# Attention pairs 3 and 4 take the VectorE turn: three pairs in place of five keep the turn on TensorE

## The chip, the cores and the metric

The kernel runs on one core of one Trainium2 chip. The metric is the time of one execution on the device, in microseconds. Three runs of the kernel before gave 651.52, 655.0 and 658.75 us; the median is 655.0 us. Besides, one execution was profiled; every row of a trace below is from that one.

## The reference

Rotary attention over 8 batches of 8 heads, 576 positions and a head width of 64, and behind it a gated feed-forward layer over the 512 features of the eight heads:

```python
q_rot, k_rot = (rotate(q), rotate(k))
scores = scale * np.matmul(q_rot, k_rot.transpose(0, 1, 3, 2))
scores = scores - np.max(scores, axis=-1, keepdims=True)
attn = np.exp(scores)
attn = attn / (np.sum(attn, axis=-1, keepdims=True) + 1e-09)
x = np.matmul(attn, v)          # the eight heads side by side: (8, 576, 512)
...
for k in range(5):              # causal taps of width 5
    gate_pre += conv_w[k][None, None, :] * xp[:, k:k + S, :]
gate = 1.0 / (1.0 + np.exp(-gate_pre))
val = x @ w_val
return (gate * val @ w_out).astype(np.float32)
```

The factors of the matrix products are split into a high and a low part, so that three products of reduced precision stand for one of float32.

## The kernel before

**Work and tiles.** Two heads make a pair; there are 32 pairs, four to a batch. A pair's steps are: load q and k (`load`, L198); rope as two multiplications by the tables and an addition (`rope_mul` L212, `rope_add` L216), then a high part on ScalarE (L223) and a low part (`qk_lo`, L227); five groups of scores on TensorE (`s_mm`, L255: four groups of 128 query rows for both heads, and one of the last 64 rows of both heads mixed, for which `q_mixed` lays out the queries); the maxima on VectorE (L261, nine) and the exponentials on ScalarE (L274, nine); the turn of the weights, so that keys lie on partitions; the product of weights and V (`pv_last` L359, `pv_mm` L369, L374, L377); the norm (`x_norm`, L405), for which reciprocal sums (L386) go out to memory and come back (L392 to L401); the high and low parts of the result (L412, L416), four taps on VectorE (L429) and one on ScalarE, and the gate (L433).

**The turn, in two kinds.** A pair p below `EARLY` (L31), and the last pair, turn on TensorE: eight groups of four transposes (`t_mm`, L303) and their edges (`th_mm`, L316), each copied out of PSUM by ScalarE (L190) or VectorE (L192). The other pairs turn on VectorE: four transposes of 32x32 blocks (`turn`, L289), and 16 DMAs on SP's queue which bring the blocks to their places (`move`, L294). The two lines that choose:

```python
ph = "e" if p < EARLY else ""
cs = TURNED.get(p, (0, 1, 2, 3) if p >= EARLY and not last else ())
```

**Feed-forward.** When the four pairs of a batch are there, two products follow (`f_mm`, L463, 192 matmuls in all for a batch), with the gate (L468) and a split (L472, L476) between them and an output copy (L482 or L484) and DMA behind them. Its weights arrive as float64 bits; eight blocks are decoded once, early on, with six steps of which five are VectorE's (L497 to L504), three matmuls (L539 to L541) and copies.

**Buffers.** PSUM holds three score buffers of two banks (`ps_s`) and two banks for all else (`ps_t`). Three buffers `big` hold turned weights, blocks on their way and raw feed-forward weights.

**What sets the order.** Every step is a job with a due time: a base (18.5 us times p, plus the step's place) plus an entry of the table `DUE`. The planner (`Plan.order`) takes the ready job with the least due time whose buffers are free. Jobs then stand on their engine's queue in that order and run in it. `PICK` gives the engine of a step where there is a choice (V VectorE, A ScalarE, G GpSimd). Early pairs have keys of their own in both tables, with an "e" behind. Where a GpSimd job follows a VectorE job which uses the port that the two share, `Plan.run` adds a wait on that job.

Of the kernel before, what the change touches and what calls it, by code (L numbers as in the profile page):

```python
# [30 lines left out]
EARLY = 5  # L31
# [113 lines left out]
def attn_gated_ffn(ctx: ExitStack, tc: tile.TileContext, q2, k2, v2, tab, w_val, conv_w, w_out, out, collect=None):  # L145
# [410 lines left out]
    def at(key, base, e, ns, fn, *args, pick=None, r="", w="", kb=0, mode=None, port=False):  # L556

        options = ns if pick else None
        if pick:
            e = PICK.get(pick, e)  # L560
            ns, port = options[e]
            args = [ENG[e] if a == "ENGINE" else a for a in args]
        plan.add(base + DUE.get(key, 0.0), e, fn, *args, r=r, w=w, port=port)
        if collect is not None:
            collect.append((key, base, pick, options, ns, kb * (3.6 if fn is move else 2.95), mode, port or e == "G"))

    def toks(f, *ranges):
        out = [f]
        for r in ranges:
            out = [x.replace("@", str(v), 1) for x in out for v in r]  # L570
        return " ".join(out)
# [30 lines left out]
    for p in range(NP):  # L602
        t = PERIOD * p
        par = p % 2
        last = p == NP - 1
        ph = "e" if p < EARLY else ""
        cs = TURNED.get(p, (0, 1, 2, 3) if p >= EARLY and not last else ())
        xt = toks(f"x{par}#@", range(5))
# [200 lines left out]
```

## Time and profile before

| | |
|---|---|
| median of three runs | 655.0 us (651.52 to 658.75) |
| the profiled execution | 652.48 us, of which the span of its instructions 650.7 us |
| TensorE, matmuls | 616.9 us busy (95% of the span) |
| VectorE | 579.1 us (89%) |
| ScalarE | 462.7 us (71%) |
| GpSimd | 390.3 us (60%) |
| DMA | 134.43 MB |
| granted TensorE clock, mean | 0.996 of full speed |

A share is an average over stages with different limits, so the rows below are read by stretch. Matmuls are pipelined and their ends are modelled; a busy TensorE need not be at its peak. Overlapping records count once in a busy time, so the mean of a step can be more than its share of the busy time.

### The profile page before, as it was taken

The page shows a single profiled execution, that of the slowest core. Times are in us where ns is not written, and L with a number is a line of the kernel's source. Part 1 is how long each engine was busy: PE and PEld are TensorE (multiplying, and loading weights), DVE is VectorE, ACT ScalarE, POOL GpSimd, SP SyncE. Part 2 cuts the span into 40 slices and gives each one's busy share as a digit, 9 for nine tenths or more (in the row PEclk, how much of TensorE's full clock was granted, in tenths as well). Part 3 has the DMA queues.
Part 4 walks back from the last instruction along what each step waited for, and adds up shares of the span by engine and source line. Part 5 has one row for each costly group of instructions (what it writes and reads, how often), then busy time and mean ns, then how long its engine had stood idle before and what let it go on. Part 6 is the DMA issues. An engine that isn't in the chain of part 4 may idle for free.

```text
span 650.7 us, 15423 instructions
## 1 busy us (share of the span) xinstructions
PE 616.9 (95%) x5683; PEld 503.4 (77%) x5683; DVE 579.1 (89%) x827; ACT 462.7 (71%) x1161; POOL 390.3 (60%) x297
## 2 busy tenths in 40 slices
PE   8899988989899998999999999999999999999997
PEld 7666665678677886888778787888788877788797
DVE  6898999998899999999999999999999999995453
ACT  4788888867777777767877777767777777664521
POOL 1322446776777868687677868766976867630200
PEclk9899999999999999999999999999999999999999
DMA  5524432378989989999999999989999898864102
GB/s 185 225 78 153 162 117 101 114 206 242 268 235 260 258 250 250 263 241 252 239 249 252 241 262 255 267 241 256 254 263 254 233 252 210 249 166 132 56 2 74
DMA packets 51482, 134.43 MB, mean 207 GB/s; under 512 B 10928, under 2 KB 20944, under 8 KB 51408
## 3 DMA queue, kind: packets, MB, share of 16 engines
q1 hardware_dynamic: 50864, 132.86, 72.8%
q8 instruction: 45, 0.74, 0.5%
q10 hardware_dynamic: 544, 0.59, 0.3%
q14 instruction: 29, 0.24, 0.1%
HBM read 62.48 MB, written 9.59 MB: 111 GB/s over the span
## 4 chain that ended last, share of the span: by engine, by line
PE 49%; DVE 23%; DMA 9%; ACT 6%; issue 4%; POOL 4%; SPq 3%; ACTq 0%; DVEq 0%; POOLq 0%
PE ps_t L463 17%; PE ps_t L369 12%; PE ps_s L255 10%; DVE nm L261 8%; DVE big L289 7%; DMA big<-big 5%; DVE g L429 3%; SPq L294 3%; ACT p L274 3%; PE ps_t L359 3%; PE ps_t L303 2%; PE ps_t L374 2%; PE ps_t L330 1%; ACT big L190 1%; DVE g L468 1%
## 5 line engine op out<-in xcount | busy, mean ns | idle before, releaser
L261 DVE TENSOR_REDUCE nm<-ps_s 128x1 f32<-128x576 f32 x288 | 201.8, 741 | 19.9 <-PE ps_s L255 18.8
L274 ACT ACTIVATE p<-ps_s,nm 128x576 f32<-128x576 f32 x256 | 187.7, 738 | 39.5 <-DVE nm L261 38.4
L255 PE MATMUL ps_s<-k,q 64*128 64x288 f32 x1536 | 145.0, 310 | 11.4 <-ACT p L274 9.2
L255 PEld LDWEIGHTS ps_s<-k,q 64*128 64x128 f32 x1536 | 111.0, 184 | 37.6 <-ACT p L274 18.2
L289 DVE STREAM_TRANSPOSE big<-p 128x1152 f32<-128x1152 f32 x104 | 139.8, 1357 | 0.0
L429 DVE SCALAR_TENSOR_TENSOR g<-x,cw,g 128x576 f32<-128x576 f32 (+1 forms) x132 | 122.4, 927 | 0.9 <-ACT g L426 0.6
L369 PE MATMUL ps_t<-big,v 128*64 128x256 f32 (+2 forms) x1024 | 118.4, 382 | 0.0
L227 POOL TENSOR_TENSOR q<-iq,q 128x576 fp32r<-128x576 f32 (+2 forms) x33 | 48.8, 1477 | 94.9 <-ACT q L223 89.8
L369 PEld LDWEIGHTS ps_t<-big,v 128*64 128x64 f32 x1024 | 70.1, 137 | 44.1 <-issue 13.5
L212 POOL TENSOR_TENSOR iq<-iq,tab 128x576 f32<-128x576 f32 x54 | 77.1, 1450 | 19.8 <-DMA iq<-in_q 13.3
L463 PE MATMUL ps_t<-yh,wout_hi 128*128 128x288 f32 x256 | 79.2, 310 | 0.0
L463 PE MATMUL ps_t<-xh,wval_hi 128*128 128x288 f32 x256 | 79.0, 309 | 0.0
L463 PE MATMUL ps_t<-yl,wout_hi 128*128 128x288 f32 x256 | 76.2, 298 | 1.9 <-POOL yl L476 1.9
L463 PE MATMUL ps_t<-xl,wval_hi 128*128 128x288 f32 x256 | 76.3, 298 | 0.0
L463 PE MATMUL ps_t<-xh,wval_lo 128*128 128x288 f32 x256 | 75.9, 297 | 0.0
L463 PE MATMUL ps_t<-yh,wout_lo 128*128 128x288 f32 x256 | 75.5, 295 | 0.0
L227 POOL TENSOR_TENSOR k<-ik,k 128x576 fp32r<-128x576 f32 x31 | 52.5, 1694 | 37.4 <-DVE iq L212 25.0
L476 POOL TENSOR_TENSOR yl<-g,yh 128x288 fp32r<-128x288 f32 x56 | 46.7, 841 | 43.5 <-ACT yh L472 41.2
L416 POOL TENSOR_TENSOR xl<-x,xh 128x576 fp32r<-128x576 f32 (+1 forms) x32 | 47.6, 1487 | 25.5 <-PE ps_t L463 13.4
L463 PEld LDWEIGHTS ps_t<-xh,wval_hi 128*128 128x128 f32 x256 | 48.7, 190 | 2.8 <-issue 1.6
L472 ACT CAST yh<-g 128x288 fp32r<-128x288 f32 x64 | 26.6, 431 | 33.9 <-DVE g L468 33.9
L463 PEld LDWEIGHTS ps_t<-yl,wout_hi 128*128 128x128 f32 x256 | 48.3, 189 | 3.1 <-POOL yl L476 3.0
(95 smaller groups left out, 1107.9 us busy)
## 6 DMA issues: line engine op xcount, KB each, us to landing
big<-big SPq DMA_DIRECT2D x416, 144.0 KB
ik<-in_k SPq DMA_DIRECT2D x31, 576.0 KB
iq<-in_q SPq DMA_DIRECT2D x31, 576.0 KB
v<-in_v SPq DMA_DIRECT2D x32, 320.0 KB
rb<-rd SPq DMA_DIRECT2D x64, 144.0 KB
out_t<-oo SPq DMA_DIRECT2D x64, 144.0 KB
big<-in_w_val SPq DMA_DIRECT2D x4, 512.0 KB
big<-in_w_out SPq DMA_DIRECT2D x4, 512.0 KB
```

The source lines that it names most:

```text
L212: eng.tensor_tensor(out=t[:, i, a:b], in0=t[:, i, a:b], in1=tabs[:, i, a:b], op=ALU.mult)
L227: eng.tensor_tensor(out=t[:, 1], in0=state[p][n + "in"][:, 0, a:b], in1=t[:, 0].bitcast(F32), op=ALU.subtract)
L255: T.matmul(out=ps[:, half, 0:288], lhsT=st["q"][rows, x, c * 128:c * 128 + 128] if c < 4 else mixq[p % 2][:, x], rhs=st["k"][rows, y, k0:k ...
L261: V.tensor_reduce(out=st[f"nm{i}"], in_=st[f"s{i}"], axis=AX.XY, op=ALU.max, negate=True)
L274: A.activation(out=pd.rearrange("p (b x) -> p b x", b=2), in_=st[f"s{i}"], func=AF.Exp, bias=st[f"nm{i}"], scale=1.0, accum_out=sums[p % 2 ...
L289: V.transpose(out=t[:, :, cs.index(c)].rearrange("p b k i -> p k b i"), in_=st[f"p{c}"].rearrange("p h s -> p (h s)").rearrange("p (k b i) ...
L369: T.matmul(out=acc[HEAD[h], 0:n], lhsT=st["v"][:, j, h, :], rhs=st["pt"][:, :, c0:c1, 5 * place(p, 2 * c0 + h) + j].rearrange("p a c i -> ...
L416: eng.tensor_tensor(out=st["xl"][:, a:b], in0=xs[p % 2][:, 4 + a:4 + b], in1=st["xh"][:, a:b].bitcast(F32), op=ALU.subtract)
L429: V.scalar_tensor_tensor(out=g, in0=x_sb[:, a + k:b + k], scalar=w, in1=g, op0=ALU.mult, op1=ALU.add)
L463: T.matmul(out=acc[:, 0:n], lhsT=wt[w][:, kc, ds], rhs=mv, start=(kc == 0 and i == 0), stop=(kc == NCH - 1 and i == 2))
L472: A.copy(out=ffn[b, "h", dc, lo], in_=ffn[b, "y", dc, lo])
L476: eng.tensor_tensor(out=ffn[b, "l", dc, lo], in0=y, in1=ffn[b, "h", dc, lo].bitcast(F32), op=ALU.subtract)
```

## The change

`EARLY` goes from 5 to 3. Pairs 3 and 4 are turned on VectorE and moved by 16 DMAs each, and take the due times and engines of the common pairs. All due times are set anew, and 17 entries of `PICK` differ. The functions stay as they are.

```diff
-EARLY = 5
+EARLY = 3
...
-DUE = {'taps': -9098.3948, 'dtap': 19.7513,
...
+DUE = {'taps': -9055.1904, 'dtap': 20.813,
...
```

What `PICK` moves: of pair 0's first-half steps, the second k multiplication, the second q multiplication and the q addition go from VectorE to GpSimd; of the early pairs, the low part of k goes from GpSimd to VectorE, the first q multiplication from VectorE to GpSimd, the mixed-query copies from ScalarE to VectorE. Of the copies behind TensorE's turn, early pairs have one 512-wide and one edge copy on VectorE (two and none before); the last pair two 512-wide and two edge copies (four and two before). The last batch's output scalings are all ScalarE's (four were VectorE's), and one low part of the last pair goes from VectorE to GpSimd.

The counts that follow: VectorE has 112 turns in place of 104; 5 copies of 512 in place of 14, and 5 edge copies of 256 in place of 2; 33 multiplications, 4 additions and 2 low parts of rope of full width in place of 37, 8 and none. The rope steps of pairs 1 to 4 on GpSimd are 20 in place of 12.

TensorE, at the product of weights and V of pair 3. Before, it stands between two score groups of pair 4 (L255), and pair 4's edge transposes (L316), its turns (L303) and a decoded weight block (L539) follow:

```order
L359 MATMUL ps_t_1275<-big_1061,v_76 64x256 x2
L359 MATMUL ps_t_1276<-big_1061,v_76 64x256 x2
L369 MATMUL ps_t_1276<-big_1061,v_76 64x256 x8
L374 MATMUL ps_t_1276<-pq_1209,v_76 64x64 x8
L377 MATMUL ps_t_1276<-pq_1209,vz 64x64 x2
L369 MATMUL ps_t_1275<-big_1061,v_76 64x256 x8
L316 MATMUL ps_t_1311<-ident,p_1186 128x128
L316 MATMUL ps_t_1311<-ident,p_1228 128x128
L303 MATMUL ps_t_1315<-ident,p_1228 128x128 x4
L303 MATMUL ps_t_1325<-ident,p_1186 128x128 x4
L539 MATMUL ps_t_1333<-wout_hi,minus 128x512
```

Now the first score groups of pair 5 stand around it (`ps_s_1333` is the last row of one, `ps_s_1396` the first of the next):

```order
L255 MATMUL ps_s_1333<-k_70,q_72 128x288
L359 MATMUL ps_t_1360<-big_1147,v_76 64x256 x2
L359 MATMUL ps_t_1361<-big_1147,v_76 64x256 x2
L369 MATMUL ps_t_1360<-big_1147,v_76 64x256 x8
L369 MATMUL ps_t_1361<-big_1147,v_76 64x256 x8
L374 MATMUL ps_t_1361<-pq_1224,v_76 64x64 x8
L377 MATMUL ps_t_1361<-pq_1224,vz 64x64 x2
L255 MATMUL ps_s_1396<-k_70,q_72 128x288
```

The transposes are gone, and the product stands one pair later in the queue of scores. The first feed-forward product stands behind the fourth score group of pair 5; before, it stood behind the third.

VectorE, in pair 3 from the maxima of its third score group on. Before: maxima (L261), two copies out of PSUM (L192), a rope addition of pair 4 (L216), a tap (L429) and two decoding steps (L497, L499):

```order
L261 TENSOR_REDUCE nm_1089<-ps_s_1004 128x1
L261 TENSOR_REDUCE nm_1107<-ps_s_1003 128x1
L192 COPY big_1061<-ps_t_1076 128x4x4x32
L216 TENSOR_TENSOR iq_881<-iq_881 128x576
L429 SCALAR_TENSOR_TENSOR g_1081<-x_84,cw,g_1081 128x576
L261 TENSOR_REDUCE nm_1132<-ps_s_1093 128x1
L261 TENSOR_REDUCE nm_1141<-ps_s_1094 128x1
L261 TENSOR_REDUCE nm_1161<-ps_s_1116 128x1
L497 TENSOR_SCALAR big_840<-big_840 128x512
L499 SCALAR_TENSOR_TENSOR big_840<-big_840 128x512
L192 COPY big_1061<-ps_t_1136 128x4x4x32
```

Now, from the same maxima on, with the four turns (L289, the first one stands ahead of these rows) and the last decoding steps (L503, L504):

```order
L261 TENSOR_REDUCE nm_1096<-ps_s_1083 128x1
L261 TENSOR_REDUCE nm_1098<-ps_s_1082 128x1
L503 TENSOR_SCALAR big_739<-big_739 128x512
L289 STREAM_TRANSPOSE big_1034<-p_1029 128x9x4x32
L504 SCALAR_TENSOR_TENSOR wout_lo<-big_739 128x512
L261 TENSOR_REDUCE nm_1129<-ps_s_1116 128x1
L261 TENSOR_REDUCE nm_1133<-ps_s_1115 128x1
L289 STREAM_TRANSPOSE big_1034<-p_1101 128x9x4x32
L289 STREAM_TRANSPOSE big_1034<-p_1131 128x9x4x32
L429 SCALAR_TENSOR_TENSOR g_1071<-x_84,cw,g_1071 128x576
L429 SCALAR_TENSOR_TENSOR g_851<-x_85,cw,g_851 128x576
L261 TENSOR_REDUCE nm_1169<-ps_s_1162 128x1
```

The copies are replaced by turns, the rope step is GpSimd's, and the decoding ends here; before, it went on into pair 5.

GpSimd, from its first step on. Before, it has the two low parts of pair 0's q (L227) and one multiplication (L212) and two low parts for each of the next pairs:

```order
L227 TENSOR_TENSOR q_71<-iq_154,q_71 128x256
L227 TENSOR_TENSOR q_71<-iq_154,q_71 128x320
L212 TENSOR_TENSOR ik_197<-ik_197,tab 128x576
L227 TENSOR_TENSOR k_70<-ik_197,k_70 128x576
L227 TENSOR_TENSOR q_72<-iq_239,q_72 128x576
L212 TENSOR_TENSOR ik_272<-ik_272,tab 128x576
L227 TENSOR_TENSOR k_69<-ik_272,k_69 128x576
```

Now it has three more steps of pair 0 ahead and between, and pair 3's steps, of the common kind, begin with `ik_454`:

```order
L212 TENSOR_TENSOR iq_150<-iq_150,tab 128x256
L216 TENSOR_TENSOR iq_150<-iq_150 128x256
L227 TENSOR_TENSOR q_71<-iq_150,q_71 128x256
L212 TENSOR_TENSOR ik_148<-ik_148,tab 128x288
L227 TENSOR_TENSOR q_71<-iq_150,q_71 128x320
L212 TENSOR_TENSOR ik_195<-ik_195,tab 128x576
L212 TENSOR_TENSOR iq_241<-iq_241,tab 128x576
L227 TENSOR_TENSOR q_72<-iq_241,q_72 128x576
L212 TENSOR_TENSOR ik_274<-ik_274,tab 128x576
L212 TENSOR_TENSOR iq_343<-iq_343,tab 128x576
L212 TENSOR_TENSOR ik_454<-ik_454,tab 128x576
L227 TENSOR_TENSOR q_71<-iq_343,q_71 128x576
```

Two steps of pair 0 stand ahead of its first low part and one behind it, ahead of the second, and pair 3's first step stands ahead of pair 2's low part (`q_71<-iq_343`).

## Rows read from the trace of the kernel before

**Rows 1.** Windows: stretch, length; PE, PEld, DVE, ACT, POOL busy; clock; DMA share, GB/s.

```profile
20.00:60.00 40.00, 38.60 (x334) 27.87 (x334) 35.29 (x65) 33.64 (x86) 11.34 (x8) 0.96 0.41 148
60.00:117.00 57.00, 51.21 (x443) 35.08 (x441) 52.53 (x76) 48.39 (x118) 27.62 (x18) 1.00 0.34 115
...
140.00:560.00 420.00, 406.60 (x3904) 336.73 (x3903) 400.75 (x541) 313.64 (x800) 313.33 (x236) 1.00 0.92 250
580.00:648.00 68.00, 65.65 (x566) 58.33 (x562) 34.64 (x63) 28.07 (x67) 5.32 (x6) 1.00 0.27 78
```

**Rows 2.** Chain of waits, in order of time: start us, us, what.

```profile
36.37 1.88 PE ps_t L369 x16
...
114.54 1.88 PE ps_t L369 x16
...
118.72 1.03 PE ps_s L255 x12
...
149.15 3.60 PE ps_t L369 x32
...
154.59 3.20 PE ps_t L463 x24
...
579.11 3.60 PE ps_t L369 x32
```

**Rows 3.** VectorE's waits, 20 to 117 us, then 140 to 560: us, times, longest.

```profile
DVE x L405 <- PE ps_t L369: 3.5, 4, 1.2
DVE nm L261 <- PE ps_s L255: 2.4, 4, 1.5
...
DVE nm L261 <- PE ps_s L255: 10.6, 22, 0.5
```

**Rows 4.** Groups by line and shape: busy us, mean ns of one | idle before, releaser.

```profile
L289 DVE STREAM_TRANSPOSE big<-p 128x1152 f32<-128x1152 f32 x104 | 139.8, 1357 | 0.0
...
L212 POOL TENSOR_TENSOR iq<-iq,tab 128x576 f32<-128x576 f32 x54 | 77.1, 1450 | 19.8 <-DMA iq<-in_q 13.3 <-DVE g L429 4.2 <-DVE nm L261 1.1
...
L303 PE MATMUL ps_t<-ident,p 128*128 128x128 f32 x192 | 30.7, 284 | 7.1 <-ACT p L274 3.0 <-ACT big L190 2.0 <-DVE big L192 0.9
...
L192 DVE COPY big<-ps_t 128x512 f32<-128x512 f32 x14 | 9.5, 685 | 3.1 <-PE ps_t L303 3.1
...
L212 DVE TENSOR_TENSOR iq<-iq,tab 128x576 f32<-128x576 f32 x8 | 5.8, 750 | 0.0
...
L192 DVE COPY big<-ps_t 128x256 f32<-128x256 f32 x2 | 0.8, 425 | 4.2 <-PE ps_t L316 4.2
...
L227 POOL TENSOR_TENSOR q<-iq,q 128x256 fp32r<-128x256 f32 x1 | 0.7, 738 | 8.0 <-ACT q L223 8.0
...
L216 DVE TENSOR_TENSOR iq<-iq 128x256 f32<-128x256 f32 x1 | 0.4, 424 | 0.0
```

**Rows 5.** Timeline of VectorE: start us, us, operation, count [idle before <-releaser].

```profile
89.28 1.96 DVE L502 SCALAR_TENSOR_TENSOR big<-big 128x512 f32<-128x512 f32 x1
...
96.10 1.97 DVE L212 TENSOR_TENSOR ik<-ik,tab 128x576 f32<-128x576 f32 x1
...
109.59 1.90 DVE L502 SCALAR_TENSOR_TENSOR big<-big 128x512 f32<-128x512 f32 x1
...
454.14 0.20 DVE L386 RECIPROCAL pm<-sums 128x9 f32<-128x9 f32 x1
454.25 0.75 DVE L429 SCALAR_TENSOR_TENSOR g<-x,cw,g 128x576 f32<-128x576 f32 x1
...
457.62 1.42 DVE L261 TENSOR_REDUCE nm<-ps_s 128x1 f32<-128x576 f32 x2 [0.49 <-PE ps_s L255]
```

**Rows 6.** Busy time by short stretches, columns as in rows 1.

```profile
16.00:20.00 4.00, 2.09 (x17) 1.26 (x14) 3.96 (x7) 2.64 (x7) 1.74 (x1) 1.00 0.95 372
20.00:24.00 4.00, 3.73 (x22) 3.07 (x22) 3.63 (x7) 3.00 (x10) 1.41 (x1) 0.65 0.62 250
...
172.00:176.00 4.00, 2.01 (x13) 1.45 (x13) 2.82 (x5) 2.99 (x7) 4.00 (x4) 1.00 1.06 269
```

More of the change, by code (lines that the diff above doesn't have):

```diff
@@ L36 @@
-PICK = {'c0': 'A', 'c0e': 'A', 'c1': 'V', 'c1e': 'V', 'c2': 'V', 'c2e': 'A', 'c3': 'A', 'c3e': 'A', 'c4': 'V', 'c4e': 'A', 'c5': 'A', 'c5e': 'A', 'c6': 'A', 'c6e': 'V', 'c7': 'V', 'c7e': 'A', 'ch0': 'A', 'ch0e': 'V', 'ch1': 'V', 'ch1e': 'A', 'chm': 'A', 'chme': 'A', 'cm': 'A', 'cme': 'A', 'kadd': 'G', 'kadd_0': 'V', 'kadd_1': 'V', 'kadde': 'V', 'kfront': 'A', 'kfronte': 'A', 'klo': 'G', 'klo_0': 'V', 'klo_1': 'V', 'kloe': 'G', 'kmul0': 'G', 'kmul0_0': 'V', 'kmul0_1': 'V', 'kmul0e': 'G', 'kmul1': 'V', 'kmul1_0': 'V', 'kmul1_1': 'V', 'kmul1e': 'V', 'od0': 'A', 'od0l': 'A', 'od1': 'A', 'od1l': 'V', 'od2': 'A', 'od2l': 'V', 'od3': 'A', 'od3l': 'A', 'qadd': 'G', 'qadd_0': 'V', 'qadd_1': 'V', 'qadde': 'V', 'qlo': 'G', 'qlo_0': 'G', 'qlo_1': 'G', 'qloe': 'G', 'qmixed': 'A', 'qmixede': 'A', 'qmul0': 'G', 'qmul0_0': 'V', 'qmul0_1': 'V', 'qmul0e': 'V', 'qmul1': 'G', 'qmul1_0': 'V', 'qmul1_1': 'V', 'qmul1e': 'V', 'xlo': 'G', 'xloe': 'G', 'xlol0': 'V', 'xlol1': 'G', 'ylo': 'G', 'ylol': 'V', 'ch3': 'V', 'ch3e': 'A', 'decout': 'A', 'decval': 'A', 'odma': 'SP', 'odmal': 'SP', 'loadk': 'SP', 'loadk_0': 'SP', 'loadk_1': 'SP', 'loadke': 'SP', 'loadq': 'SP', 'loadq_0': 'SP', 'loadq_1': 'SP', 'loadqe': 'SP', 'loadv': 'SP', 'loadve': 'SP', 'mv0': 'SP', 'mv1': 'SP', 'mv2': 'SP', 'mv3': 'SP', 'rr': 'SP', 'rre': 'SP', 'rw': 'SP', 'rwe': 'SP'}
@@ new lines @@
+PICK = {'c0': 'A', 'c0e': 'A', 'c1': 'A', 'c1e': 'A', 'c2': 'A', 'c2e': 'A', 'c3': 'V', 'c3e': 'A', 'c4': 'A', 'c4e': 'A', 'c5': 'A', 'c5e': 'A', 'c6': 'A', 'c6e': 'A', 'c7': 'V', 'c7e': 'V', 'ch0': 'A', 'ch0e': 'V', 'ch1': 'V', 'ch1e': 'V', 'chm': 'A', 'chme': 'A', 'cm': 'A', 'cme': 'A', 'kadd': 'G', 'kadd_0': 'V', 'kadd_1': 'V', 'kadde': 'V', 'kfront': 'A', 'kfronte': 'A', 'klo': 'G', 'klo_0': 'V', 'klo_1': 'V', 'kloe': 'V', 'kmul0': 'G', 'kmul0_0': 'V', 'kmul0_1': 'V', 'kmul0e': 'G', 'kmul1': 'V', 'kmul1_0': 'G', 'kmul1_1': 'V', 'kmul1e': 'V', 'od0': 'A', 'od0l': 'A', 'od1': 'A', 'od1l': 'A', 'od2': 'A', 'od2l': 'A', 'od3': 'A', 'od3l': 'A', 'qadd': 'G', 'qadd_0': 'G', 'qadd_1': 'V', 'qadde': 'V', 'qlo': 'G', 'qlo_0': 'G', 'qlo_1': 'G', 'qloe': 'G', 'qmixed': 'A', 'qmixede': 'V', 'qmul0': 'G', 'qmul0_0': 'V', 'qmul0_1': 'V', 'qmul0e': 'G', 'qmul1': 'G', 'qmul1_0': 'G', 'qmul1_1': 'V', 'qmul1e': 'V', 'xlo': 'G', 'xloe': 'G', 'xlol0': 'G', 'xlol1': 'G', 'ylo': 'G', 'ylol': 'V', 'ch3': 'V', 'ch3e': 'A', 'decout': 'A', 'decval': 'A', 'odma': 'SP', 'odmal': 'SP', 'loadk': 'SP', 'loadk_0': 'SP', 'loadk_1': 'SP', 'loadke': 'SP', 'loadq': 'SP', 'loadq_0': 'SP', 'loadq_1': 'SP', 'loadqe': 'SP', 'loadv': 'SP', 'loadve': 'SP', 'mv0': 'SP', 'mv1': 'SP', 'mv2': 'SP', 'mv3': 'SP', 'rr': 'SP', 'rre': 'SP', 'rw': 'SP', 'rwe': 'SP'}
```

2 lines of the change are left out of this document (1 added, 1 removed).

## The prediction

> **What bounds the kernel now.** I read the page's busy shares first: TensorE and VectorE lie close together, and neither share says which one sets the time, because the stages differ. So I went on to the busy time by stretch [rows 1]. From 140 to 560 us VectorE works 400.75 of 420 us and TensorE 406.60: both are full, with 19.2 us of VectorE idle (4.6%). From 20 to 117 us, where pairs 0 to 4 run, VectorE works 35.29 + 52.53 = 87.8 of 97 us, so 9.2 us are idle, and GpSimd works only 11.34 + 27.62 = 39.0 us. The DMA share is 0.34 to 0.41 there and 0.92 later. In the last stretch, 580 to 648 us, VectorE is half idle and TensorE works 65.65 of 68 us: the tail is TensorE's.
>
> The chain of waits [rows 2] gives the pace, because each pair's product of weights and V stands in it. Pair 0's begins at 36.37 us and pair 4's at 114.54: (114.54 - 36.37) / 4 = 19.5 us a pair. Pair 5's begins at 149.15 and pair 29's at 579.11: 429.96 / 24 = 17.9 us a pair. The early pairs are slower by 1.6 us each although they carry no part of the feed-forward product, and the reader should see why: VectorE also does their rope steps and the decoding of eight weight blocks. VectorE's waits [rows 3] agree: in the early pairs it waits for TensorE's product (3.5 us) and scores (2.4 us); in the steady part 22 waits, 10.6 us, are for scores. One of them is shown, of 0.49 us at 457.62 [rows 5]: it is the second score group of a pair, which stands behind the product of weights and V in TensorE's queue.
>
> So up to about 579 us the time is VectorE's work plus its waits, and what follows is TensorE's tail. I make the sum on VectorE.
>
> **The change, part by part.** The profiled execution took 652.5 us (span 650.7); the median of the runs shown is 655.0, that is 2.5 more. Differences are worked out on the former and added to the latter.
>
> 1. VectorE's work. Two pairs more are turned there: 8 transposes at 1357 ns [rows 4], +10.9 us. Their copies out of PSUM go: 512-wide copies on VectorE fall from 10 to 3 in the early pairs, -7 x 0.685 = -4.8; 256-wide ones rise from none to 3, +3 x 0.425 = +1.3. The mixed-query copies of three pairs come to VectorE, six of 64x128, a shape which the trace shows on ScalarE alone; between the 0.20 of a reciprocal [rows 5] and the 0.425 of a 256-wide copy I take 0.3, since it lies between them in size: +1.8. Rope: pairs 1 to 4 had five steps each there (20); now pairs 1 and 2 have five and pairs 3 and 4 one (12): -8 x 0.75 = -6.0. Three half-width steps of pair 0 go to GpSimd: -3 x 0.43 = -1.3. Sum: +1.9 us. In the last pair and the output, VectorE loses two 512-wide copies and four output scalings where it is half idle; that is worth nothing.
>
> 2. TensorE's work. 64 transposes of weights and 8 of their edges go, at 30.7 / 192 = 0.16 us each: 11.5 us of busy time. I cost this at nothing. TensorE has nothing to put there: the feed-forward products need the normalised output of pairs 0 to 3, and their first one stands behind pair 5's fourth score group, where it stood behind its third. From pair 9 on the two queues stand alike but for a few neighbours. ScalarE loses the copies out of PSUM too; it stands in no term above.
>
> 3. Waits of the early pairs. Pairs 3 and 4 now wait as turned pairs do. Of 60 to 117 us 4.5 are idle (57 - 52.53); at the steady 4.6% it would be 2.6: -1.9. Bounds: nothing, and the same for the whole early stretch, 9.2 - 4.5 = -4.7.
>
> 4. GpSimd's load. It gains eight rope steps of 1450 ns and the three halves of pair 0, of 0.74 by the nearest row: 11.6 + 2.2 = 13.8 us more in the early stretch. Where both engines run, VectorE's steps with two operands in SBUF get long: between 89 and 112 us three such steps took 1.96, 1.97 and 1.90 us [rows 5], and the plain rope step is 0.75. That is 5.83 - 3 x 0.75 = 3.6 us of lengthening beside 27.6 us of GpSimd work, 0.13 per us; 13.8 x 0.13 = +1.8. Bounds: nothing, and twice that. The Trainium skill says why, in "SBUF — State Buffer" (section "SBUF: two separate sides"): the two engines share a pair of ports that is locked for a whole instruction, so that the later one blocks. By that rule the sum would lie anywhere up to the full 13.8 us; the rows show a part of it.
>
> 5. The start. GpSimd now does four steps of pair 0 in a row (q multiply, q add, q low part, k multiply), and VectorE's k add waits for the last of them. Three of the steps were VectorE's: 3 x (0.74 - 0.42) = +1.0. Bounds: nothing, and twice that, if the waits between the engines count too.
>
> 6. The steady pairs. The same work in nearly the same order. The reciprocal moves into the wait behind the second normalisation; 22 waits, each shortened by the 0.11 between the start of a reciprocal and of the next step (454.14 to 454.25, [rows 5]), would give -2.4 if VectorE alone set the pace. It shares it with TensorE, so I take half: -1.2. Bounds: 0 and -2.4.
>
> 7. The queues. SP issues 32 moves more and DMA carries them; the share there is at most 0.41 and rises to the steady 0.92 at worst, which the steady pairs bear at 17.9 us. The product of pair 3 waits for its 16 moves, but pair 4's work on VectorE lies between. Nothing. The tail gives at most 68 - 65.65 = 2.35 and can lose as much through the new order of pair 31; I take nothing.
>
> Sum: +1.9 - 1.9 + 1.8 + 1.0 - 1.2 = **+1.6**, so 654.1 on the profiled execution and **656.6 us** on the median: no change that a measurement can tell. I use 1% (6.5 us) as that bound; the runs shown differ by as much.
>
> **The rivals.**
>
> *A. Faster.* The decoding now ends within pair 3 and no longer reaches pair 5, so most of it could run where GpSimd is least busy (11.34 of 40 us). Then the lengthening of 3.6 us goes instead of growing, the whole early stretch takes on steady waits (-4.7), and the reciprocal gives its full 2.4: 655.0 + 1.9 - 4.7 - 3.6 - 2.4 = 646.2. For it: the early pace of 19.5. Against it: GpSimd's added steps begin with pair 1, exactly there, and VectorE has as much to do as before.
>
> *B. Slower, by TensorE's clock.* Between the product of pair 2 and the first feed-forward product TensorE now has only score groups (1.03 us each for twelve matmuls), two small transposes a pair and the product of pair 3. In this trace the granted clock stood at half (1.2 GHz) once: after 16 to 20 us, with TensorE busy 2.09 of 4 us, the next stretch shows 0.65 [rows 6]. Against it: 172 to 176 us with 2.01 busy kept 1.00. At half clock a score group takes up to 1.03 more and the product 3.6 more. About five of the thirteen groups are followed by only two maxima and a turn and would be waited for: 5 x 1.03 + 3.6 = 8.8, so 656.6 + 8.8 = 665.4. It decides the case from 4.9 us on: the product and two groups waited for at half clock. The Trainium skill's "TensorE: Matmul & The Clock Gate" (section "Why this matters for your kernels") advises against idle gaps between bursts of matmuls for this reason; by that rule the drop would come, and the trace agrees at one of two places.
>
> *C. Slower, by a backlog.* The products of pairs 3 and 4 stood before pair 5's second score group; now they stand behind the first group of pairs 5 and 6, where the feed-forward work is. That puts one product more, 4.4 us with its small parts (from 149.15 to 154.59, less a score group of 1.03), into a stretch after which TensorE is idle 13.4 of 420 us. If that idle time can't be used, the delay stays to the end: 656.6 + 4.4 = 661.0.
>
> **How the numbers follow.** Forecast 0.54, A 0.22, B 0.14, C 0.10. Faster by over 1% (below 648.5): 0.20 of A and 0.02 of the forecast's edge, 0.22. Slower (above 661.5): B's 0.14, half of C and 0.02 of the forecast's edge, 0.21. Within 1%: 0.57. The forecast's own range comes from the bounds: low 655.0 + 1.9 - 4.7 + 0 + 0 - 2.4 = 649.8, high 655.0 + 1.9 + 0 + 3.6 + 2.0 + 0 = 662.5. The whole range reaches into A and B so far that about 0.1 is left out at each end: 648 to 665.
>
> **What would show it.** Step 1: VectorE's busy time within 3 us of 579. Step 3: idle time of VectorE between the fourth and fifth pair near 2.6 us in 57. Step 4: more early steps of about 1.9 us among the decoding lines. Step 5: the first maximum of pair 0 about 1 us later. Step 6: fewer than 10.6 us of waits for scores in the steady part, at 17.8 to 17.9 us a pair. Rival B shows as a granted clock below 1 between 80 and 125 us, C as TensorE without idle time from 120 to 200 us and VectorE waiting for it. The forecast is wrong if the product of pair 29 begins more than 6 us away from 579.

## The result, and the profile after

The changed kernel takes 650.6 us (median of 10 runs, 643.3 to 655.1), the kernel before 656.0 us (10 runs): a ratio of 0.9889, with a 95% interval of 0.985 to 0.993. It is faster by 1.1%, where I forecast no change (656.6 against 655.0). In a later session on one chip it took 645.5 us against 654.7, a ratio of 0.986 (0.980 to 0.992). The profiled execution of after is at its median (650.4, span 648.5), that of before was 3.5 us below its own.

Busy time by stretch after the change, to be laid beside [rows 1] (us of stretch, then busy time of TensorE, its weight loads, VectorE, ScalarE, GpSimd, granted clock, DMA share, GB/s):

```profile
20.00:60.00 40.00, 34.92 (x276) 25.09 (x276) 36.94 (x70) 32.66 (x78) 12.56 (x9) 0.96 0.42 149
60.00:117.00 57.00, 45.62 (x324) 30.53 (x324) 49.75 (x67) 40.09 (x96) 33.82 (x23) 0.81 0.48 146
140.00:560.00 420.00, 411.15 (x3986) 342.33 (x3984) 404.24 (x551) 323.38 (x813) 319.83 (x240) 1.00 0.92 254
580.00:648.00 68.00, 62.64 (x536) 56.14 (x532) 28.72 (x52) 28.24 (x66) 6.35 (x6) 1.00 0.24 70
```

Two things differ. The granted clock in 60 to 117 us is 0.81 instead of 1.00: rival B's sign. In 140 to 560 us both TensorE and VectorE are a little busier per microsecond, since the same work is done in less time. The short stretches show where the clock is half (compare [rows 6]):

```profile
96.00:100.00 4.00, 3.06 (x22) 2.12 (x20) 4.00 (x5) 2.51 (x7) 1.58 (x2) 1.00 0.04 15
100.00:104.00 4.00, 0.62 (x3) 0.30 (x3) 4.00 (x7) 1.90 (x6) 1.40 (x1) 0.79 0.79 184
104.00:108.00 4.00, 3.27 (x17) 2.45 (x19) 3.76 (x6) 4.00 (x10) 3.27 (x3) 0.50 0.99 234
```

The chain of waits has the products (start, us, what; compare [rows 2]): pair 2's, pair 3's, which takes 3.89 us instead of 3.60 since it begins at half clock (up to 119.4 us), and pair 29's at 576.26 instead of 579.11.

```profile
83.27 2.87 PE ps_t L369 x16
...
118.84 3.89 PE ps_t L369 x32
...
576.26 3.60 PE ps_t L369 x32
```

VectorE's waits (us, times, longest), 20 to 117 us and then 140 to 560 (compare [rows 3]): early, the waits for scores grew from 2.4 to 6.9 us and those for the product fell from 3.5 to 1.7; in the steady part the waits for scores did not shrink (10.6 to 11.1 us).

```profile
DVE nm L261 <- PE ps_s L255: 6.9, 9, 1.6
DVE x L405 <- PE ps_t L369: 1.7, 2, 1.2
...
DVE nm L261 <- PE ps_s L255: 11.1, 31, 0.5
```

What shrank in the steady part is VectorE's work. These are its groups between the first maximum of pair 10 and that of pair 31, first before (202.4 to 579.0 us), then after (206.6 to 576.9); after the shapes stand the count, the busy us and the mean ns of one:

```profile
L429 DVE SCALAR_TENSOR_TENSOR g<-x,cw,g 128x576 f32<-128x576 f32 x84 | 82.4, 982 | 0.0
L212 DVE TENSOR_TENSOR ik<-ik,tab 128x576 f32<-128x576 f32 x21 | 18.1, 864 | 0.0
L386 DVE RECIPROCAL pm<-sums 128x9 f32<-128x9 f32 x21 | 4.0, 190 | 0.0
```

```profile
L429 DVE SCALAR_TENSOR_TENSOR g<-x,cw,g 128x576 f32<-128x576 f32 x85 | 73.9, 869 | 0.0
L212 DVE TENSOR_TENSOR ik<-ik,tab 128x576 f32<-128x576 f32 x21 | 19.5, 930 | 0.0
L386 DVE RECIPROCAL pm<-sums 128x9 f32<-128x9 f32 x21 | 4.3, 203 | 0.0
```

L429 is the convolution's tap, four a pair on VectorE. The same taps take 869 ns instead of 982. Since VectorE runs its instructions in order, the time from one of its instructions to a later one is the sum of its work and its idle time in between; I worked that out from its records for both stages, overlaps of neighbours taken off (us). A pair's stretch begins with its first maximum; only pair 0's is counted from its second, 0.7 us later in all three traces:

| VectorE | before | after | after, second trace |
|---|---|---|---|
| second maximum of pair 0 at | 14.5 | 14.8 | 14.6 |
| **pair 0 to pair 10** | 188.0 | 191.8 | 189.9 |
| idle | 15.1 | 14.7 | 12.8 |
| turns | 25.6 | 35.9 | 35.9 |
| copies out of PSUM and mixed-query copies | 6.3 | 6.7 | 6.7 |
| rope | 18.5 | 14.7 | 14.7 |
| decoding | 25.4 | 23.5 | 23.8 |
| **pair 10 to pair 31** | 376.6 | 370.3 | 367.9 |
| idle | 14.2 | 14.0 | 12.0 |
| taps | 75.9 | 66.7 | 66.6 |
| k's multiply | 16.5 | 17.9 | 17.9 |
| **pair 31 to the last output copy** | 68.7 | 67.7 | 67.7 |

So the early part lost 3.8 us and 0.3 at the start (2.1 in all in the second trace: 14.6 + 189.9 - 14.5 - 188.0, less rounding), the steady part gained 6.3 (8.7), of it 9.2 from the taps, and the tail gained 1.0 up to the last output copy; what follows that copy took 3.0 us before and 3.9 after (2.8 in the second trace), so that the spans differ by 2.2. Three other traces with the order of before (e3, e7 and e9 below, which move at most one step of the turned pairs) took 379.8, 382.5 and 380.7 us in the steady part, with 75.0 to 77.9 of taps: the profiled execution of before was a short one, and the usual gain there is nearer 11 us. Against these three, idle time shrank, too, from 17.7 to 19.0 us to 14.0 and 12.0. Part of that are VectorE's waits for the read-back of the row sums: 1.6 to 5.4 us between 240 and 560 us in the four traces with that order, none in the two after.

### The profile page after: what moved, and what is told of

It is laid out like the page before. It is cut to its first block, busy times and chain, and to the rows that moved or that the text cites. A ratio compares the mean times of both kernels' runs of the same rounds, so it can differ in the third digit from the quotient of the medians.

```text
span 648.5 us, 15339 instructions
## 1 busy us (share of the span) xinstructions
PE 611.0 (94%) x5611; PEld 500.6 (77%) x5611; DVE 571.2 (88%) x819; ACT 463.6 (71%) x1145; POOL 404.6 (62%) x309
## 4 chain that ended last, share of the span: by engine, by line
PE 65%; DVE 11%; DMA 7%; POOL 5%; ACT 4%; issue 3%; SPq 3%; ACTq 0%; DVEq 0%; POOLq 0%
PE ps_t L463 23%; PE ps_s L255 16%; PE ps_t L369 14%; DVE nm L261 4%; DMA big<-big 3%; DVE big L289 3%; SPq L294 3%; PE ps_t L359 3%; PE ps_t L303 2%; DMA iq<-in_q 2%; PE ps_t L374 2%; DMA v<-in_v 2%; ACT p L274 2%; PE ps_t L330 2%; POOL yl L476 2%
## 5 line engine op out<-in xcount | busy, mean ns | idle before, releaser
L261 DVE TENSOR_REDUCE nm<-ps_s 128x1 f32<-128x576 f32 x288 | 204.6, 746 | 24.0 <-PE ps_s L255 23.8
L255 PE MATMUL ps_s<-k,q 64*128 64x288 f32 x1536 | 146.9, 317 | 13.3 <-ACT p L274 9.7
L289 DVE STREAM_TRANSPOSE big<-p 128x1152 f32<-128x1152 f32 x112 | 150.9, 1361 | 0.0
L255 PEld LDWEIGHTS ps_s<-k,q 64*128 64x128 f32 x1536 | 112.7, 190 | 38.9 <-ACT p L274 19.9
L369 PE MATMUL ps_t<-big,v 128*64 128x256 f32 (+2 forms) x1024 | 119.4, 385 | 0.0
L429 DVE SCALAR_TENSOR_TENSOR g<-x,cw,g 128x576 f32<-128x576 f32 (+1 forms) x132 | 111.0, 843 | 1.5 <-ACT g L426 1.2
L212 POOL TENSOR_TENSOR iq<-iq,tab 128x576 f32<-128x576 f32 (+1 forms) x61 | 86.4, 1436 | 40.9 <-DVE g L429 8.9
L476 POOL TENSOR_TENSOR yl<-g,yh 128x288 fp32r<-128x288 f32 x56 | 48.8, 872 | 48.2 <-ACT yh L472 48.2
L227 POOL TENSOR_TENSOR q<-iq,q 128x576 fp32r<-128x576 f32 (+2 forms) x33 | 56.9, 1725 | 34.5 <-ACT q L223 30.6
L463 PE MATMUL ps_t<-xh,wval_lo 128*128 128x288 f32 x256 | 75.9, 296 | 0.0
L216 POOL TENSOR_TENSOR iq<-iq 128x576 f32<-128x576 f32 (+1 forms) x30 | 41.7, 1388 | 49.5 <-DVE g L429 43.2
L227 POOL TENSOR_TENSOR k<-ik,k 128x576 fp32r<-128x576 f32 x29 | 41.5, 1430 | 17.0 <-ACT k L223 5.3
```

What stands on the lines that cost most here:

```text
L212: eng.tensor_tensor(out=t[:, i, a:b], in0=t[:, i, a:b], in1=tabs[:, i, a:b], op=ALU.mult)
L216: eng.tensor_tensor(out=t[:, 0], in0=t[:, 0], in1=t[:, 1], op=ALU.add)
L227: eng.tensor_tensor(out=t[:, 1], in0=state[p][n + "in"][:, 0, a:b], in1=t[:, 0].bitcast(F32), op=ALU.subtract)
L255: T.matmul(out=ps[:, half, 0:288], lhsT=st["q"][rows, x, c * 128:c * 128 + 128] if c < 4 else mixq[p % 2][:, x], rhs=st["k"][rows, y, k0:k ...
L261: V.tensor_reduce(out=st[f"nm{i}"], in_=st[f"s{i}"], axis=AX.XY, op=ALU.max, negate=True)
L289: V.transpose(out=t[:, :, cs.index(c)].rearrange("p b k i -> p k b i"), in_=st[f"p{c}"].rearrange("p h s -> p (h s)").rearrange("p (k b i) ...
```

## The experiments

**One part of the table at a time.** (The edits are told in words, the tables being long.) The due times fall into three sets: steps of early pairs with the weights, steps of turned pairs with their feed-forward products, and steps of the last pair with the last batch. Each run takes one set from the changed kernel and the rest from before.

```diff
 e1_steady: EARLY = 5, DUE of the turned pairs from after, all others from before
 e2_early:  EARLY = 3, DUE and PICK of the early pairs from after, all others from before
 e3_tail:   EARLY = 5, DUE and PICK of the last pair and batch from after, all others from before
```

> The kernel before (five early pairs) with the due times of the changed kernel for the steps that only the turned pairs and their feed-forward products have; early pairs and last pair as before. Theory S (the gain is in the order of the turned pairs, 0.30 us a pair over pairs 10 to 31 in the two traces, and the early part of the changed kernel costs about 4 us): 655.96 - 6.3 = 649.7 us, with VectorE's taps near 843 ns as in the changed kernel, where they were 927 before. Theory E (the gain comes from pairs 3 and 4 being turned): no change, 655 to 657. My forecast's step on the steady pairs would give 654.8.

> The other half: pairs 3 and 4 turned and the early steps' due times and engines of the changed kernel, with the due times of before for the turned pairs and for the last pair. Theory S: slower by the 4 us that the traces show lost by the end of pair 10, 660 us, with the granted clock at half for stretches between 80 and 135 us. Theory E: faster, near 650. My forecast's steps without the one on the steady pairs: 655.96 + 2.8 = 658.8.

> The kernel before with only the changed kernel's due times and engines for the last pair and the last batch's feed-forward products. Between the first maximum of pair 31 and the last output the traces differ by 1.0 us, so theory S expects 655 us; my forecast took nothing, 656. If the order of the last batch is worth the 2.35 us of TensorE's idle time in the tail, 653.6.

Measured: 681.4 us (ratio 1.039, 1.035 to 1.043), 673.7 (1.026, 1.022 to 1.031) and 659.2 (1.005, 1.002 to 1.009). No expectation held for the whole, and no part of the table gains anything alone. The first two lose where early pairs meet turned ones: in e1 the first maximum of pair 9 comes 25.9 us later than before, with waits of VectorE of 5.5 and 4.0 us for the products of pairs 5 and 6; in e2 that of pair 5 comes 16.3 us later. The due times of both kinds of pairs interleave in the same queues, and mixed tables seem to put steps in each other's way. The last pair is a second seam: from the first maximum of pair 31 to the last output copy e3 takes 73.0 us and e1 75.9, where before took 68.7. In e3 that is more than the whole loss (2.6 us by the medians). Behind the first seam e1 shows what was asked: from pair 12 to pair 30 it takes 314.2 us, where before took 320.5 and after 315.9. Its taps take 57.2 us there, as in after (57.2), against 64.2 before. The gain belongs to the order of the turned pairs. What the seam costs in detail I did not follow further.

**Switching the order in the middle of like pairs**, and two candidates alone:

```diff
+SWITCH = 12
+LATE = {...}      # e5: all steps of turned pairs; e6: khi, klo, qadd, qmul0, qmul1; e7: rr
...
-        plan.add(base + DUE.get(key, 0.0), e, fn, *args, r=r, w=w, port=port)
+        plan.add(base + due[0].get(key, 0.0), e, fn, *args, r=r, w=w, port=port)
...
+        due[0] = {**DUE, **LATE} if p >= SWITCH else DUE
```

> The kernel before, in which only pairs 12 to 30 take the changed kernel's due times for the steps of turned pairs (first to twelfth pair and last pair as before), so that the two orders meet in the middle of like pairs. Theory S (the order of the turned pairs is what gained): from pair 12 on 0.45 us a pair are gained, the slope seen between pair 10 (+27.0) and pair 29 (+18.4) in the run with these due times from pair 5 on; 19 x 0.45 = 8.6, so about 648 us. My forecast's step on the steady pairs: 655.6. Theory E (turning pairs 3 and 4 gained): 656.6, no change.

> The kernel before, in which from pair 12 on five due times are the changed kernel's: k's rounding on ScalarE and k's low part, q's two multiplies and q's add on GpSimd. In the order GpSimd's k low part then stands behind the first tap and q's add behind the third, where each stood ahead of it and ran beside it. Theory P (the gain is that GpSimd's steps no longer run beside VectorE's taps): tap 1 falls from 1.27 us to about 0.9 and tap 3 from 0.99 to 0.9, 0.45 us a pair less on VectorE, 18 pairs, so 648 to 650 us. Theory R (the gain is the earlier read-back of the row sums): 656.6, since its due times stay.

> The kernel before, in which from pair 12 on the read-back of the inverse row sums has the changed kernel's due time, 4 us earlier, so that it no longer stands behind the output transfers on SP's queue in one pair of four. Theory R: the waits of the normalisation for the read-back (1.6 us in 200 to 560 us in the profile of before, 4.9 and 4.1 in two later runs with the same order) go, 652 to 655 us, and taps stay long. Theory P: no change, 656 to 657.

Measured: e5 679.4 us (1.039, 1.034 to 1.044). This seam, too, costs: the first maximum of pair 13 is 15.1 us late, with one wait of 5.4 us; the tail costs 7.2 us again (75.9). From pair 17 to pair 30 the run takes 228.7 us, after 228.8, before 231.7 and e3, with the order of before, 232.7; the taps take 41.2, 41.1, 46.6 and 47.2. That is the gain again, and again in the taps.

e7 took 656.7 us against 655.1 (1.0005, 0.997 to 1.004). Its edit did not do what it was meant to: in its trace VectorE waits 4.7 us for the read-back between 240 and 560 us, where before waited 1.6. So the earlier due time alone gains nothing, and what it is worth that these waits are gone in the changed kernel was not tested.

e6 took 676.6 us (1.035, 1.030 to 1.039): 21 us slower where theory P expected 7 faster. But it says more for the mechanism than a gain would have. GpSimd's q add now waits for the third tap (431.67), as planned, and therefore runs beside the fourth. VectorE, then GpSimd, in e6 (start, us, operation; a bracket holds the idle time before it):

```profile
431.67 0.76 DVE L431 SCALAR_TENSOR_TENSOR g<-x,cw,g 128x576 f32<-128x576 f32 x1
432.34 0.75 DVE L214 TENSOR_TENSOR ik<-ik,tab 128x576 f32<-128x576 f32 x1
433.01 1.97 DVE L431 SCALAR_TENSOR_TENSOR g<-x,cw,g 128x576 f32<-128x576 f32 x1
```

```profile
432.57 1.79 POOL L218 TENSOR_TENSOR iq<-iq 128x576 f32<-128x576 f32 x1 [2.81 <-DVE g L431]
```

The fourth tap takes 1.97 us where an undisturbed one takes 0.76. The collision was moved, not removed: from pair 12 to 30 the four taps of a pair went from 1.21, 0.87, 0.99 and 0.81 us on average to 1.35, 1.15, 0.83 and 1.97. Over these pairs the taps took 89.7 us instead of 64.2, and the stretch 347.3 instead of 320.5: 25.5 of the 26.8 us lost are tap time.

In the changed kernel these four are 0.89, 0.87, 0.91 and 0.81 us. So the first tap gains most, 0.32 of 0.40 us a pair, and the third 0.08. Beside the first tap before ran GpSimd's low part of k, 0.64 us a pair on average; after, it begins 0.9 to 1.4 us behind the tap's start and runs beside maxima and other steps. Before, then after, VectorE's first tap and GpSimd's low part (L227):

```profile
424.06 2.06 DVE L429 SCALAR_TENSOR_TENSOR g<-x,cw,g 128x576 f32<-128x576 f32 x1
424.08 1.42 POOL L227 TENSOR_TENSOR k<-ik,k 128x576 fp32r<-128x576 f32 x1 [0.34 <-ACT k L223]
```

```profile
424.67 0.80 DVE L429 SCALAR_TENSOR_TENSOR g<-x,cw,g 128x576 f32<-128x576 f32 x1
426.10 1.43 POOL L227 TENSOR_TENSOR k<-ik,k 128x576 fp32r<-128x576 f32 x1
```

The tap of before begins 0.02 us ahead of the low part and is still the one that waits. At another pair it begins 0.06 us ahead, and then GpSimd's step waits instead and the tap loses nothing:

```profile
352.98 0.80 DVE L429 SCALAR_TENSOR_TENSOR g<-x,cw,g 128x576 f32<-128x576 f32 x1
353.04 2.04 POOL L227 TENSOR_TENSOR k<-ik,k 128x576 fp32r<-128x576 f32 x1 [0.35 <-ACT k L223]
```

The third tap's neighbour is q's add. Compare one place in before and after. Before, q's add (365.16) starts under the third tap and both it and k's multiply are stretched; it is the only one of 18 pairs in which the multiply takes over 1 us. First VectorE, then GpSimd:

```profile
364.50 1.32 DVE L429 SCALAR_TENSOR_TENSOR g<-x,cw,g 128x576 f32<-128x576 f32 x1
365.74 1.97 DVE L212 TENSOR_TENSOR ik<-ik,tab 128x576 f32<-128x576 f32 x1
367.63 0.81 DVE L429 SCALAR_TENSOR_TENSOR g<-x,cw,g 128x576 f32<-128x576 f32 x1
```

```profile
365.16 1.93 POOL L216 TENSOR_TENSOR iq<-iq 128x576 f32<-128x576 f32 x1
```

After, the third tap stands two maxima ahead of k's multiply, q's add waits 0.76 us for it and then runs beside the maxima, which read PSUM:

```profile
363.89 1.03 DVE L429 SCALAR_TENSOR_TENSOR g<-x,cw,g 128x576 f32<-128x576 f32 x1
364.84 1.41 DVE L261 TENSOR_REDUCE nm<-ps_s 128x1 f32<-128x576 f32 x2
366.18 0.92 DVE L212 TENSOR_TENSOR ik<-ik,tab 128x576 f32<-128x576 f32 x1
```

```profile
365.06 1.41 POOL L216 TENSOR_TENSOR iq<-iq 128x576 f32<-128x576 f32 x1 [0.76 <-DVE g L429]
```

So the 1.41 us of GpSimd's add lie mostly under 1.41 us of maxima, and neither got longer. The add's end reaches into k's multiply, which on average grew from 0.82 to 0.93 us. I read from this that it takes both halves, a GpSimd step that waits and a VectorE neighbour that does not collide with it; e6 had only the first.

**The reciprocal**, my step 6, in before's table. The first run took the changed kernel's due time, which among before's other due times put the reciprocal two maxima too late; the second put it where the changed kernel has it.

```diff
-'rinv': 21.1103
+'rinv': 23.5322      # e4_rinv
+'rinv': 23.0         # e9_rinv2
```

> The kernel before with one due time changed, that of the reciprocal of the turned pairs, which moves behind the second normalisation. If that is the whole gain of the turned pairs: 649.7 us. By my forecast's bounds: 653.6 to 656.0. If it delays the reciprocals' way through DRAM to the next product, slower than 656.

> The kernel before with one due time changed, that of the reciprocal, set so that in the steady pairs it stands right behind the second normalisation and ahead of the next maximum, where the changed kernel has it (the run with the changed kernel's own due time put it two maxima later, and TensorE waited 15.7 us for it). My forecast's step on the steady pairs (the reciprocal fills a wait): 652.7 to 655.1. If TensorE's queue waits for the later reciprocal here too, with its two transposes and what stands behind them: slower, 660 or more. If it plays no part, 655 to 656.

Measured: e4 676.1 us (1.031, 1.027 to 1.036), e9 657.7 (1.002, 1.000 to 1.005). The reciprocal's place gains nothing. Two maxima later it costs 20 us, because TensorE's transposes of the sums (L345) wait for it, and score groups and feed-forward products stand behind them (TensorE in e4, 200 to 560 us: us, times, longest):

```profile
PE ps_t L345 <- DVE pm L386: 15.7, 9, 1.9
```

**One collision put back, and all waits taken away**, in the changed kernel:

```diff
-'khi': 20.2265, 'klo': 6.063
+'khi': 18.32, 'klo': -3.9259                    # e10_klo, as before
...
-            if i in self.behind:                # e11_noport
-                tc.add_manual_dep(made[i], made[self.behind[i]].name, wait, reason="port")
```

> The changed kernel with two due times of before, k's rounding and k's low part, for the turned pairs: ScalarE's rounding moves ahead of one neighbour and GpSimd's k low part no longer waits for the first tap but for the fourth tap of an earlier pair, as before. Theory P (what the turned pairs gained is the time by which taps beside GpSimd's steps grow longer; over six runs the pace of a pair followed the sum of the taps and k's multiply): tap 1 rises from 0.89 to about 1.2 us, so 0.3 to 0.4 us a pair over 25 pairs, 658 to 660 us. Rival: the change in the order of the other engines gained, and the taps only came with it: 650 to 652.

> The changed kernel without the planner's waits of GpSimd's steps behind VectorE's taps and multiplies (order as it is). Theory P: more of GpSimd's steps run beside the taps, the taps grow, and the pace of a pair in 300 to 560 us grows by as much as taps and k's multiply together; with tap lengths of 1.2 us for two of the four, +0.6 us a pair, 665 us. Rival: the waits (22.8 us of GpSimd's time in 280 to 560 us) only hold GpSimd back, whose low parts TensorE waits for (3.2 us): faster, 648.

Measured: e11 659.2 us against 655.9 for before, so about 8.6 above the changed kernel (11 by the two ratios). In its trace, pair 12 to 30, the taps grow from 57.2 to 62.6 us (the third from 0.91 to 1.16 us, beside q's add), k's multiply falls from 15.4 to 12.0, and the stretch takes 317.7 instead of 315.9 (313.5 in the second trace). The direction is theory P's, the size, 0.1 to 0.2 us a pair, well under the 0.6 that I expected; most of the rest of the 8.6 is not in this trace's steady part (its first maximum of pair 10 comes 4.7 us later than the changed kernel's), and I did not follow it.

e10 took 708.5 us (1.079, 1.074 to 1.083): 58 us above the changed kernel for two due times, which move k's rounding by one neighbour on ScalarE. Theory P gives only a part. Tap 1 went from 0.89 to 1.53 us and the taps of pairs 12 to 30 from 57.2 to 65.9. The rest is idle time, 51.1 us instead of 11.8, and the chain of waits shows the loop (start, us, what):

```profile
432.72 7.68 DMA big<-big
...
441.53 3.60 PE ps_t L369 x32
...
445.71 1.03 PE ps_s L255 x12
446.74 0.76 DVE nm L261
...
447.53 1.55 ACT p L274 x4
449.08 0.58 ACT k L223
...
449.73 1.71 POOL k L227
...
451.46 0.36 SPq L198
...
453.69 8.65 DMA big<-big
```

A product waits for its moves; the scores behind it release a maximum and exponentials; k's rounding stands behind these on ScalarE; GpSimd's k low part waits for the rounding; SP's load of the next k (L198) waits for the low part, which frees its buffer; and the next four moves stand behind that load. One round takes 21 us (432.72 to 453.69) instead of 17.6. In the changed kernel the load stands behind those four moves (SP's queue, start, us, operation):

```profile
391.30 2.42 SPq L294 DMA_DIRECT2D big<-big  x4
393.81 0.53 SPq L198 DMA_DIRECT2D ik<-in_k  x1
```

The planner puts it ahead of them as soon as its own order frees the buffer earlier, which the low part's new place does.

One table holds those that bear on the turned pairs: VectorE from the first maximum of pair 12 to that of pair 30 (us).

| kernel | stretch | taps | k's multiply | idle | rest |
|---|---|---|---|---|---|
| before | 320.5 | 64.2 | 13.3 | 13.0 | 230.0 |
| e3, e7, e9 (its order) | 323.1, 324.3, 324.4 | 64.4, 67.8, 65.8 | 13.9, 13.9, 12.0 | 14.9, 12.8, 15.9 | 229.9, 229.8, 230.7 |
| after | 315.9 | 57.2 | 15.4 | 11.8 | 231.5 |
| e13, e14 (its order) | 313.5, 313.5 | 57.0, 56.9 | 15.4, 15.3 | 9.8, 9.6 | 231.3, 231.7 |
| e1 (its order of turned pairs) | 314.2 | 57.2 | 15.5 | 10.0 | 231.5 |
| e11 | 317.7 | 62.6 | 12.0 | 11.8 | 231.3 |
| e6 | 347.3 | 89.7 | 14.5 | 12.9 | 230.2 |
| e4 | 339.0 | 64.9 | 12.0 | 30.1 | 232.0 |
| e10 | 364.5 | 65.9 | 15.0 | 51.1 | 232.5 |

The rest is the same within 2.7 us; a change of order acts through collisions on the taps or through waits.

**TensorE's clock**, by matmuls that nothing reads, in the changed kernel:

```diff
+        for _ in range(KEEP...):      # e8: 12 behind each score group of pairs 2 to 5
+            T.matmul(out=tiles[0][:, 1, 288:416], lhsT=minus, rhs=minus, start=True, stop=True)
```

> The changed kernel with twelve more matmuls of 128 columns behind each score group of pairs 2 to 5, into columns of the score banks that nothing reads, so that TensorE is busier between 80 and 135 us. If the half clock there (rival B) costs what the traces show lost by pair 10, 4 us: the granted clock stays at 1.00 and the time falls to about 646.5. If the clock falls because of something else, or VectorE's waits there are for the moves by DMA: 650 to 652, and the products of pairs 2 and 3 as late as they were (83.3 and 118.8 us).

> The changed kernel with matmuls that nothing reads only where TensorE is idle in its trace: 24 behind pair 4's first score group (idle from 99.07 to 102.60 us), 10 behind pair 3's third (89.45 to 91.44), 6 each behind pair 4's second and third, 0.11 us each by the run before this one. If the half clock from 102.8 to 119.8 us is what makes VectorE wait for scores there (five waits of 0.9 to 1.55 us), the clock stays at 1.00 there and the time falls by 3 to 5 us, to 646 or 647. If the clock falls all the same, or the pace there is set by something else, 650 to 653.

Measured: e8 676.8 us (1.033), e12 653.2 (0.996, 0.992 to 0.999). The clock fell in both. In e8 the added matmuls stand ahead of the next scores in TensorE's queue. In e12 TensorE was busy 3.44 and 3.16 of 4 us ahead of the fall at 104.4 us; the added matmuls fill the changed kernel's idle 3.53 us there (from 99.06), and idle times of 0.71 and 1.00 us behind them (from 102.77 and 103.87) were left:

```profile
96.00:100.00 4.00, 3.44 (x23) 2.54 (x24) 4.00 (x6) 3.02 (x8) 2.80 (x2) 1.00 0.50 195
100.00:104.00 4.00, 3.16 (x25) 2.81 (x25) 4.00 (x7) 1.06 (x4) 0.57 (x1) 1.00 0.56 130
104.00:108.00 4.00, 3.13 (x18) 2.85 (x18) 2.23 (x4) 3.36 (x7) 3.22 (x3) 0.55 1.02 237
```

So neither run tests what the half clock costs; both are inconclusive.

**Is the early loss VectorE's work?** The changed kernel again, and with copies moved back to ScalarE:

```diff
-'qmixede': 'V'
+'qmixede': 'A'                    # e14_mixed, e15_mixed_copy
-'c7e': 'V'
+'c7e': 'A'                        # e15_mixed_copy
```

> The changed kernel unchanged, for a second trace and for the same chip as the next two. By VectorE's account of the first traces (work plus idle time from one first maximum to another): pair 0 to pair 10 near 191.8 us, where before took 188.0; pair 10 to pair 31 near 370.3 us, of it 66.7 of taps, where traces with the order of before took 376.6 to 382.5, of it 75 to 78 of taps. Whole: 648 to 653 us. If the difference of the steady stretch were chance of one execution, this trace would show it near 376.

> The changed kernel with the mixed-query copies of the three early pairs back on ScalarE, as before; in VectorE's account of the early stretch they cost 3.6 us (six copies, two of them 1.43 and 1.49 us, the others 0.22), where my forecast had 1.8. Theory W (the early stretch is VectorE's work, and the half clock costs nothing there, since VectorE's idle time is 14.7 us against 15.1): 3.6 us less up to pair 10, 647 us. Rival B (TensorE at half clock sets the early pace): VectorE's idle time grows by what its work shrinks, 650 to 651.

> As the run before it, and the early pairs' copies of the eighth transposes out of PSUM also on ScalarE (three of 128x512, 0.685 us each): by theory W 2.1 us more off VectorE's early work, 645 us; by rival B no change, 650. If ScalarE's queue becomes late for the exponentials: slower than the run before it.

Measured on one chip: e13 645.5 us, e14 645.6, e15 651.3 (against 654.7 for before). e13 confirms the steady part in a second execution (367.9 us, taps 66.6). e14 takes 3.6 us of copies from VectorE and gains nothing that shows: up to pair 10 it takes 190.6 us where e13 took 189.9 (and the first trace 191.8), with 16.7 us of idle time instead of 12.8 (14.7). That speaks against theory W, with one trace of e14 and medians too loose to exclude 3 us. Idle time that grows as work shrinks is what I had named for rival B; it does not tell the half clock from other causes of waiting. e15 is slower than e14; in its trace the first maximum of pair 0 comes 3.0 us later, 1.0 us more is lost up to pair 10 and 3.2 from there to pair 31; I did not settle why. None of the runs beats the changed kernel.

## Why the prediction was wrong

**Step 6 is the step that failed.** I took the steady pairs as "the same work in nearly the same order", worth -1.2 us, at most -2.4, and saw only the reciprocal. They gave -6.3 us against the profiled execution of before, -8.7 in the second trace, some 11 against the other traces with that order. The reciprocal's place is worth nothing (e9), the waits for scores did not shrink, and what did is the taps, 9.2 us (against the other traces also 4 to 7 us of idle time). The rows for it stood in the trace: a tap is 0.76 us undisturbed, and four taps a pair took 982 ns on average. I had even priced this lengthening, but in step 4 and for the early stretch alone, where three steps of 1.9 us caught the eye [rows 5]. Between 89 and 112 us there is a fourth long step that I left out, and it is a tap:

```profile
103.09 1.70 DVE L429 SCALAR_TENSOR_TENSOR g<-x,cw,g 128x576 f32<-128x576 f32 x1
```

In the steady part the lengthening was 84 x (0.982 - 0.76) = 18.6 us, five times as much as the 3.6 that I had for the early one. I should have asked of the few neighbours that changed on GpSimd and VectorE which of them run beside each other.

The rule that I cited in step 4, of the Trainium skill's "SBUF — State Buffer" (section "SBUF: two separate sides"), is the one at work: whichever of the two engines starts first holds the shared ports for its whole instruction. The traces agree in that one of the two runs at its own length and the other gets longer: in e6 a tap that starts under q's add takes 1.97 us, and 25.5 of the 26.8 us lost from pair 12 to 30 are taps. Which of the two is first the records do not always show (0.02 and 0.06 us in the rows above).

**Steps 1 to 5** came out close in size: +2.8 forecast up to the steady pairs, +0.3 for the start and +3.8 up to pair 10 measured (2.1 in all in the second trace). That is luck, since inside they were not right. Turns +10.3 (10.9 forecast) and copies -3.2 (-3.5, from [rows 4]) held; the mixed-query copies cost 3.6 instead of 1.8, since two of six took 1.43 and 1.49 us and the others 0.22; rope gave back 3.8 of 6.0 (the halves of pair 0 lie ahead of this stretch). Step 4's lengthening left the decoding (-1.9 us) and went to the rope steps that stayed (0.71 to 0.82 us each). Step 3's waits: 15.1 to 14.7, and 12.8 in the second trace, where I had -1.9. Step 5 was +0.3 for +1.0. And e14 speaks against adding up VectorE's work in that stretch at all: 3.6 us taken away came back as idle time in its trace. **Step 2** held for work, but its TensorE time was not free of effect: its idle time is where the clock falls. **Step 7** held: the tail gave 1.0 up to the last output copy, and 0.1 to the end of the span (1.2 in the second trace).

**Rival B happened** and did not decide. I gave it 0.14; the clock was at half from 102.3 to 119.4 us, and in three shorter stretches between 82 and 133. The waits that it named are there: in the second trace, VectorE's maxima of pair 4 wait 1.00 and 1.55 us for score groups at half clock:

```profile
107.94 1.42 DVE L261 TENSOR_REDUCE nm<-ps_s 128x1 f32<-128x576 f32 x2 [1.00 <-PE ps_s L255]
...
112.20 1.42 DVE L261 TENSOR_REDUCE nm<-ps_s 128x1 f32<-128x576 f32 x2 [1.55 <-PE ps_s L255]
```

I priced it at 8.8 us. The waits for scores between 14 and 140 us grew by 6.0 (2.9 to 8.9; 7.3 in the first trace), but VectorE's other waits there, for products and for transposes, fell from 6.3 to 1.7 (4.3). What the early part would take at full clock stays open. **Rival A** came nearer to the time (646.2) for the wrong reasons: steady waits and the reciprocal gave nothing. **Rival C** did not happen: the first maximum of pair 6 was 3.2 us late and that of pair 10 4.2, and by pair 29 nothing of it was left.

Of the signs I had named, VectorE's busy time was outside (571.2 us, not within 3 of 579), and that was the one to read: it fell although turns were added. The product of pair 29 was inside (576.26), since the early loss hid part of the gain.

## What to carry to other kernels

When a change reorders a full engine, go through what each moved instruction runs beside on the engines that share something with it, and price that from the spread of one instruction's duration (0.76 to 2.06 us here), not from its mean. Moving one collision away is worth nothing if the step lands beside the next victim. And a list of due times that belongs together is hard to judge, or to take over, key by key: one key, two and five, exchanged alone between the two tables, cost 20, 58 and 21 us here (e4, e10, e6), the first two through an in-order queue in which something late had come to stand first, the third through a new collision.

## What was unexpected of the hardware

A copy of 64x128 within SBUF on VectorE took 0.22 us four times and 1.43 and 1.49 us twice. The two long ones run beside a multiply of 1.42 us on GpSimd (copies at 15.67 and 53.19 us, multiplies at 15.59 and 53.18), the short ones beside nothing there. Whether TensorE's clock falls could not be read here from its busy time in the 4 us ahead: 3.44 and 3.16 of 4 us were followed by half clock in e12, while before had 2.01 of 4 at full clock [rows 6].
